# Top-k attention and Fourier mixing: in the first batch, the copies of P and the attention's pieces come a step later and the weight conversion comes last in ScalarE's step

## The chip, the cores and the metric

The kernel runs on one core of one Trainium2 chip, in float32. The metric is device microseconds of a whole execution. The core has a matrix engine (TensorE, PE), three engines for elementwise work (VectorE or DVE, ScalarE or ACT, GpSimd or POOL), and queues for DMA, nearly all of them issued by SyncE (SP).

## The reference, cut to what matters

```python
# attention: q, k, v of (8 batches, 8 heads, 576 tokens, 64)
scores = scale * np.matmul(q, k.transpose(0, 1, 3, 2))
kth = np.partition(scores, -32, axis=-1)[..., -32:-31]
scores = np.where(scores >= kth, scores, -1000000000.0)
attn = softmax(scores)
attn_out = np.matmul(attn, v)
# x: (8, 576, 512), heads side by side
mixed = np.real(fft(fft(x, axis=1), axis=2))
u = x + mixed
un = (u - mean(u)) / np.sqrt(var(u) + 1e-06)
out = u + np.maximum(un @ w_ch1, 0.0) @ w_ch2
```

w_ch1 has 512 x 2048 elements, w_ch2 2048 x 512. The weights arrive as 64-bit floats, which the kernel turns into float32 itself.

## The kernel before

**Tiles and steps.** The heads of a batch are worked in four pairs. A pair has nine tiles of query rows in the order `IN_PAIR` (line 301): for each head four tiles of 128 rows, and one that holds the last 64 rows of both heads. There are 288 tiles, and one loop (line 1394) runs over steps `i`, each of which issues different stages of several tiles; 36 tiles make a batch (`PER_BATCH`). The schedule is manual: every engine works its instructions in the order in which this loop writes them. Lists by step (`plan`, filled by `at(step, where, fn)`) hold the work that does not follow the tiles: weights, the Fourier transform, sums. A queue of matrix units of the last part (`mlp_units`) is drawn from between the fixed pieces by a budget per step; it is empty until batch 0 has been transformed.

**One tile.** `scores` (line 309) lets TensorE multiply q and k into two PSUM banks of the tag "sp" (two buffers) and ScalarE copy them to SBUF as S (L372), and in a second part the last 64 keys, the "tails" (L339, copies L343). `top_ops` (375) gives VectorE four rounds of the eight largest (L393) and their removal (L395); in step i it does rounds 2 and 3 of tile i interleaved with rounds 0 and 1 of tile i + 1. `bounds` (398) makes the tile's bounds on GpSimd (nt, L402). `mask` (406): ScalarE's relu (L409), then GpSimd's subtraction (L412). `expo` (414): ScalarE's exp with the row sum (L418), which reads what the subtraction wrote. `transposes` (423): TensorE turns P by blocks of 128 into one or two PSUM banks of the tag "tp" (two buffers; L439, L450, L454), and ScalarE copies them into PT (L442, L451, L455, L457). `attend` (461) multiplies PT with v (L476, 20 matmuls) in pieces: after tile 1 of a pair 128 columns, after tile 4 the other 192, after tiles 6 and 8 128 each. `attended` (482) copies the result to xT and prepares the reciprocals of the row sums (L490, L495, L502); `to_tokens` (507) turns it back (L516) and leaves the normalisation into x to VectorE (L503, L520, L527). `prep` (269) turns q or k of the next pair (L283; ScalarE's copies L291, L293, L297), q in step 0 of a pair (in step 2 for the first), k in step 5.

**The weights in batch 0.** 32 chunks of 128 x 512 come in by DMA (L186), five ahead; nearly every step of the first 34 works one. ScalarE makes three conversions (`convert`: L191, L207, L210), VectorE shifts the chunk of L191 (L199, `shift`, issued after round 3 of tile i), GpSimd joins the parts: L218 ahead of the mask's subtraction, L220 after it. In steps 19 and 27 (and 36 and 37) `centre` (1246) lets TensorE form column means in another bank of the tag "sp" (L1250). ScalarE copies the mean in the list "convert" of the next step (L1263), and GpSimd subtracts it from columns of the weights (L1259) in the four steps after.

**A step of the first batch** (`short`, steps 1 to 36). The loop issues, in this order: the conversions of step i; exp of tile i - 1; scores of the tile three ahead, and after them what `attended` left from the step before; preparations; means; score tails; transposes of tile i - 1 with their copies; `to_tokens`; the attention piece if tile i - 1 ends one; VectorE's rounds with the shift; the bounds and the mask of tile i. So ScalarE's order is: conversions (i), exp (i - 1), score copies, preparation, tails, copies of P (i - 1), relu (i). Later batches put the stages in other places, by the branches without `short`.

Of the kernel before, what the change touches and what calls it, by code (L numbers as in the profile page):

```python
# [18 lines left out]
P = 128  # L19
# [53 lines left out]
def kernel(  # L73
# [9 lines left out]
    nc = tc.nc  # L83
# [6 lines left out]
    NF = NC - 1  # L90
    TAIL = 2 * TH
# [10 lines left out]
    CW = (2 * P + TAIL, 2 * P)  # L102
# [199 lines left out]
    PER_PAIR = len(IN_PAIR)  # L302
# [117 lines left out]
            accum_out=den_t[pair % 3][:, c:c + 1],  # L420
        )

    def transposes(i):


        pair, t, e = items[i]
        p_sb = Wk.pop(i)
        ch, col = CHUNK_OF[t]
        if (pair, ch) not in PT:
            PT[pair, ch] = attp.tile(  # L430
                [P, 2 * NF + 1, CW[ch]], F32, name=f"PT_{pair}_{ch}", tag=f"PT{ch}", bufs=1
            )
        pt = PT[pair, ch]

        def full():
            k0 = TAIL if e == 1 else 0
            tp = ps_t.tile([P, 4, P], F32, name=f"tpP_{i}", tag="tp")
            for c in range(NF):
                nc.tensor.transpose(tp[:, c, :], p_sb[:, k0 + P * c:k0 + P * (c + 1)], ident)  # L439
            dsts = [(e, 0, P)] if e is not None else [(0, 0, TAIL), (1, TAIL, TAIL)]  # L440
            for he, o, w in dsts:
                nc.scalar.copy(  # L442
                    out=pt[:, NF * he:NF * (he + 1), col:col + w], in_=tp[:, :, o:o + w]
                )

        def tails():
            tp = ps_t.tile([P, 4, P], F32, name=f"tpP_{i}_t", tag="tp")
            if e == 1:
                both = Wp.pop(i - 1).rearrange("p e s -> p (e s)")[:, NF * P:S + TAIL]
                nc.tensor.transpose(tp[:, 0, :], both, ident)  # L450
                nc.scalar.copy(out=pt[:, 2 * NF, col:col + P], in_=tp[:, 0, :])  # L451
                return
            Wp.pop(i)
            nc.tensor.transpose(tp[:, 0, :], p_sb[:, S - P:S], ident)  # L454
            nc.scalar.copy(out=pt[TAIL:P, 2 * NF, col:col + TAIL], in_=tp[TAIL:P, 0, TAIL:P])  # L455
            for r in (0, TH):
                nc.scalar.copy(  # L457
                    out=pt[r:r + TH, 2 * NF, col:col + TAIL],
                    in_=tp[TAIL + r:TAIL + r + TH, 0, 0:TAIL],
                )  # L460

        full()
        if e != 0:
            tails()
        return 0.48 if e == 0 else 0.6

    def attend(pair, ch, c0=0, c1=None):

        c1 = CW[ch] if c1 is None else c1
        pt, vv = PT[pair, ch], v_of[pair]  # L470
        if c0 == 0:
            o_of[pair, ch] = ps_o.tile([P, CW[0]], F32, name=f"o_{pair}_{ch}", tag="o")
        o = o_of[pair, ch]
        for c in range(NC):
            for e in range(2):
                nc.tensor.matmul(  # L476
                    o[D * e:D * (e + 1), c0:c1],
                    lhsT=vv[:, c, e, :],
                    rhs=pt[:, 2 * NF if c == NF else NF * e + c, c0:c1],
                    start=(c == 0),  # L480
                    stop=(c == NC - 1),
                )
        return (c1 - c0) / 115.0
# [866 lines left out]
        at(arrivals[-1], "units", lambda b=b: (queue if b else waiting).extend(mlp_units(b)))  # L1350

    queue, waiting, pending, written, now, out_next = [], [], [], set(), [0], []
    step_us = 6.0

    def fixed_cost(i):
# [19 lines left out]
    def run(i, where):  # L1375
        for fn in plan.pop((i, where), []):
            fn()
# [16 lines left out]
    while i < N + 4 or plan or queue or sums:  # L1394
        now[0] = i
        run(i, "begin")
        pair_of = i // PER_PAIR

        short = 0 <= i - 1 < PER_BATCH
        done = i - 1 if short else i - 2 if PER_BATCH <= i - 2 < N else None  # L1400

        fixed, j = [], i + 3
        e = items[j][2] if j < N else None
        preps = []

        q_step = i == 2 if pair_of == 0 else i % PER_PAIR == 0
        if i < N and q_step:
            preps.append(lambda: prep("q", pair_of + 1))  # L1410
        if i < N and i % PER_PAIR == 5:
            preps.append(lambda: prep("k", pair_of + 1))
        fixed.append(lambda: scores(j - 1, 1) if e == 1 else scores(j, 0))
        n_mask = 0
        fixed += preps

        tok = []

        if pending and pending[0][0] <= i and (
            i < 2 * PER_BATCH + 4 or (i - 3) % PER_PAIR not in (4, 8)  # L1420
        ):
            _, pp, pc = pending[0]
            if pp // NPB < 2 or pp // NPB - 2 in written:
                pending.pop(0)
                tok.append(lambda: to_tokens(pp, pc, not short))
        if not short:
            fixed += tok
        for where in ("pe1", "pe2", "pe"):
            fixed += plan.pop((i, where), [])
        if e is None and j < N:  # L1430
            fixed.append(lambda: scores(j, 1))
        n_tr = len(fixed)
        if done is not None:
            fixed.append(lambda: transposes(done))
        if short:
            fixed += tok
            pair, r = divmod(i - 1, PER_PAIR)
            piece = {1: (0, 0, P), 4: (0, P, CW[0]), 6: (1, 0, P), 8: (1, P, CW[1])}.get(r)
            if piece is not None:
                fixed.append(lambda: attend(pair, *piece))  # L1440
            if i == PER_BATCH:
                fixed.append(lambda: attended(NPB - 1, 1, late_next) or 0.0)
                fixed.append(lambda: to_tokens(NPB - 1, 1, False))
        if i in arrivals:
            carry = min(carry, 0.0) if i > arrivals[0] else -5.0
            run(i, "units")
            step_us = level(i)
        room = step_us - carry - fixed_cost(i)
        cost, got = carry, 0.0
        run(i, "convert")  # L1450
        if short:
            expo(i - 1)
        for n, fn in enumerate(fixed):
            cost += fn()
            if n == n_mask:
                if PER_BATCH <= i - 1 < N:
                    mask(i - 1)
                run(i, "act")
                for fn in out_next:
                    fn()  # L1460
                out_next.clear()
            if n == min(n_tr, len(fixed) - 1) and PER_BATCH <= i - 1 < N:
                expo(i - 1)

            got += some(max(room * (n + 1) / len(fixed) - got, 1.1 if fn in preps else 0.0))
        if short:
            if piece is not None and r in (4, 8) and i < PER_BATCH:

                out_next.append(lambda pc=(pair, r // 8): attended(*pc, late_next))
                pending.append((i + 1, pair, r // 8))  # L1470

        soon_tile = 2 * PER_BATCH - 1
        for tile in (i - 3, i - 2):
            if not PER_BATCH <= tile < N or (tile == i - 2) != (tile == soon_tile):
                continue
            pair, r = divmod(tile, PER_PAIR)
            if r in (4, 8):
                cost += attend(pair, r // 8)
                attended(pair, r // 8, late_next)
                pending.append((i + 1, pair, r // 8))  # L1480
        if i < N:
            if q_step:
                load_nat("k", pair_of + 1)
            if i % PER_PAIR == 5:
                load_nat("q", pair_of + 2)
            if i % PER_PAIR == 6:
                load_v(pair_of + 1)
        first, second = top_ops(i, (2, 3)), top_ops(i + 1, (0, 1))
        for n in range(max(len(first), len(second))):
            for ops in (first, second):  # L1490
                if n < len(ops):
                    ops[n]()
                if ops is first and n == len(first) - 1:
                    run(i, "shift")
        if not first:
            run(i, "shift")

        planned = 1.5 * len(plan.get((i, "pool0"), [])) + 1.3 * len(plan.get((i, "pool2"), []))
        run(i, "pool0")
        some_sums(max(2.1 - planned, 0.0))  # L1500
        bounds(i)

        some_sums(1.3)
        if i < PER_BATCH:
            mask(i, lambda: run(i, "join"))
        for fn in late_now:
            fn()
        run(i, "dve")
        for where in ("pool", "pool2", "load", "load2"):
            run(i, where)  # L1510
        late_now[:] = late_next
        late_next.clear()
        carry = max(-4.0, min(4.0, cost + got - step_us))
        i += 1
# [36 lines left out]
```

## Time and profile before

| | |
|---|---|
| median of three runs | 1907.68 us (lowest 1907.42) |
| the profiled execution | 1907.16 us, of it the span 1905.4 us |
| TensorE busy (PE) | 1790.4 us, 94% |
| VectorE busy (DVE) | 1585.3 us, 83% |
| ScalarE busy (ACT) | 1208.5 us, 63% |
| GpSimd busy (POOL) | 908.4 us, 48% |
| relu L409, exp L418 of ScalarE, one each | 787 ns, 780 ns |
| subtraction L412 of GpSimd | 1416 ns |
| joins L218, L220 of GpSimd (first 220 us) | 1290 ns, 1298 ns |
| conversions L191, L207, L210 (first 220 us) | 663, 669, 665 ns |
| shift L199 of VectorE (first 220 us) | 608 ns in the mean, 32 times |

How to read it: busy time is a sum over the whole execution. Lines of a timeline give the start in us from the span's start, the duration in us, the engine, the line of the kernel, the operation, what it writes and what it reads; a bracket at the end gives how long the engine had been idle and what ended that. PEld is TensorE's loading of weights, beside the matmuls. Records of one engine may overlap by some tenths of a microsecond[...]: the starts, not the durations, give the rate.

### The profile page before, as it was taken

Reading aid. Unit: us, or ns where it says so; the run is one execution under the profiler, and the core shown is the slowest. Engines: PE = TensorE matmul, PEld = TensorE weight load, DVE = VectorE, ACT = ScalarE, POOL = GpSimd, SP = SyncE. Lnnn points to the kernel's source line nnn. Section 1 sums busy time; section 2 is a strip of 40 time slices with the busy share of each in tenths; the row PEclk is TensorE's granted clock in tenths of the full one; section 3 lists DMA queues with packets and bytes.
Section 4 is the critical chain, followed back from the end, with each engine's and each line's share of the span. In section 5 each row is a group of like instructions: output and inputs, shape, how many; then the busy total and the mean of one; then the engine's idle time right before and its main releaser. Section 6 shows DMA issues by size and latency. Waiting matters only on the chain.

```text
span 1905.4 us, 28704 instructions
## 1 busy us (share of the span) xinstructions
PE 1790.4 (94%) x9200; PEld 1182.4 (62%) x9200; DVE 1585.3 (83%) x3301; ACT 1208.5 (63%) x3078; POOL 908.4 (48%) x1278
## 2 busy tenths in 40 slices
PE   5567799999899999999999999999999999999999
PEld 3344465474567756667567656667567656667678
DVE  7999999999899999989899888989899888872110
ACT  6878657776766767657676667666676667652100
POOL 4768643556535374345534464245534464241022
PEclk7787899999999999999999999999999999999999
DMA  5333001311104111131113101141113102030132
GB/s 165 104 94 108 20 13 50 99 56 25 41 14 130 34 25 47 42 107 28 25 47 98 53 20 52 35 114 27 25 47 97 53 19 57 25 103 6 50 101 80
DMA packets 184342, 111.25 MB, mean 58 GB/s; under 512 B 125952, under 2 KB 174208, under 8 KB 184192
## 3 DMA queue, kind: packets, MB, share of 16 engines
q1 hardware_dynamic: 183408, 109.20, 20.3%
q8 instruction: 74, 1.21, 0.3%
q14 instruction: 76, 0.62, 0.1%
q10 hardware_dynamic: 784, 0.21, 0.0%
HBM read 93.63 MB, written 15.73 MB: 57 GB/s over the span
## 4 chain that ended last, share of the span: by engine, by line
PE 80%; ACT 8%; DVE 6%; POOL 3%; issue 1%; DMA 1%; SPq 1%; POOLq 0%; DVEq 0%; ACTq 0%
PE hp L878 26%; PE cp L905 10%; PE o L476 8%; PE tpP L439 6%; PE sp L369 5%; PE cw L1075 5%; PE cv L1075 4%; PE yp L667 3%; PE cp L944 3%; DVE m L393 2%; DVE wk L395 2%; PE sp_t L339 2%; PE mp L728 2%; POOL wk L412 1%; ACT wk L409 1%
## 5 line engine op out<-in xcount | busy, mean ns | idle before, releaser
L412 POOL TENSOR_TENSOR wk<-S,wk 128x576 f32<-128x576 f32 x288 | 407.7, 1416 | 731.8 <-ACT wk L409 701.2
L393 DVE MAX8 m<-wk 128x8 f32<-128x576 f32 x864 | 626.3, 749 | 6.1
L878 PE MATMUL hp<-unT,w 128*128 128x256 f32 (+1 forms) x2048 | 539.9, 410 | 2.6 <-ACT unT L796 2.6
L878 PEld LDWEIGHTS hp<-unT,w 128*128 128x128 f32 x2048 | 374.3, 191 | 124.7 <-issue 25.8
L395 DVE MATCH_REPLACE8 wk<-m,wk 128x576 f32<-128x576 f32 x576 | 427.6, 742 | 0.0
L418 ACT ACTIVATE wk<-wk,nt 128x576 f32<-128x576 f32 x288 | 224.7, 780 | 75.6 <-POOL wk L412 74.5
L409 ACT ACTIVATE wk<-S,nt 128x576 f32<-128x576 f32 x288 | 226.8, 787 | 36.2 <-POOL nt L402 35.2
L439 PE MATMUL tpP<-ident,wk 128*128 128x128 f32 x1152 | 183.9, 284 | 67.3 <-ACT wk L418 40.7
L905 PE MATMUL cp<-w,hT 128*128 128x512 f32 x512 | 240.6, 598 | 0.0
L442 ACT COPY PT<-tpP 128x512 f32<-128x512 f32 (+1 forms) x320 | 171.2, 547 | 106.8 <-PE tpP L439 104.3
L393 DVE MAX8 m<-S 128x8 f32<-128x576 f32 x288 | 214.0, 743 | 21.6 <-ACT S L343 21.6
L439 PEld LDWEIGHTS tpP<-ident,wk 128*128 128x128 f32 x1152 | 141.2, 145 | 141.2 <-ACT wk L418 64.2
L882 ACT ACTIVATE hT<-hp 128x320 f32<-128x320 f32 (+1 forms) x256 | 104.7, 409 | 194.5 <-PE hp L878 192.1
L395 DVE MATCH_REPLACE8 wk<-m,S 128x576 f32<-128x576 f32 x288 | 213.7, 742 | 0.0
L476 PE MATMUL o<-PT,v 128*64 128x256 f32 (+3 forms) x1440 | 195.2, 414 | 1.9 <-ACT PT L442 1.8
L372 ACT COPY S<-sp 128x512 f32<-128x512 f32 (+1 forms) x264 | 141.7, 588 | 48.9 <-PE sp L369 48.6
L369 PE MATMUL sp<-kT,qT 64*128 64x512 f32 (+1 forms) x528 | 160.2, 666 | 4.8 <-ACT means L1263 3.3
L476 PEld LDWEIGHTS o<-PT,v 128*64 128x64 f32 x1440 | 111.4, 152 | 73.8 <-issue 16.7
L905 PEld LDWEIGHTS cp<-w,hT 128*128 128x128 f32 x512 | 88.8, 190 | 86.3 <-issue 86.2
L1020 POOL TENSOR_TENSOR hT<-hT 128x512 f32<-128x512 f32 x64 | 81.4, 1275 | 100.3 <-ACT hT L882 88.6
L1075 PE MATMUL cw<-w,hT 128*128 128x256 f32 x448 | 106.7, 383 | 1.4 <-POOL nt L402 1.2
L1075 PEld LDWEIGHTS cw<-w,hT 128*128 128x128 f32 x448 | 81.4, 190 | 18.9 <-issue 5.2
(157 smaller groups left out, 2179.3 us busy)
## 6 DMA issues: line engine op xcount, KB each, us to landing
w<-w_parts SPq DMA_DIRECT2D x82, 512.0 KB, 4.4
space<-in_moe_w_ch_dram SPq DMA_DIRECT2D x32, 512.0 KB, 3.5
nat<-in_q_dram SPq DMA_DIRECT2D x128, 64.0 KB, 2.1
v<-in_v_dram SPq DMA_DIRECT2D x128, 64.0 KB, 2.2
out_dram<-x SPq DMA_DIRECT2D x32, 256.0 KB, 2.1
nat<-in_k_dram SPq DMA_DIRECT2D x124, 64.0 KB, 2.2
w_parts<-w_t SPq DMA_DIRECT2D x8, 512.0 KB, 2.9
w_s<-w_parts SPq DMA_DIRECT2D x8, 512.0 KB, 4.8
```

Of the source, the lines that this page charges most:

```text
L369: nc.tensor.matmul(sp[r], lhsT=qT[hd, q_cols], rhs=kT[hd, :], start=True, stop=True)
L393: ops.append(lambda src=src, m8=m8: nc.vector.max(out=m8, in_=src))
L395: ops.append(lambda src=src, m8=m8: nc.vector.match_replace(w, m8, src, NEG))
L409: nc.scalar.activation(out=w, in_=Ssb[i], func=AF.Relu, scale=-FAR, bias=Nt[i][:, 1:2])
L412: nc.gpsimd.tensor_tensor(out=w, in0=Ssb.pop(i), in1=w, op=ALU.subtract)
L418: nc.scalar.activation(out=w, in_=w, func=AF.Exp, bias=Nt.pop(i)[:, 0:1], accum_out=den_t[pair % 3][:, c:c + 1],)
L439: nc.tensor.transpose(tp[:, c, :], p_sb[:, k0 + P * c:k0 + P * (c + 1)], ident)
L442: nc.scalar.copy(out=pt[:, NF * he:NF * (he + 1), col:col + w], in_=tp[:, :, o:o + w])
L476: nc.tensor.matmul(o[D * e:D * (e + 1), c0:c1], lhsT=vv[:, c, e, :], rhs=pt[:, 2 * NF if c == NF else NF * e + c, c0:c1], start=(c == 0), ...
L878: nc.tensor.matmul(hp[:, 0:w], lhsT=w1[:, dt, P * it:P * (it + 1)], rhs=unT[:, dt, 0:w], start=(dt == 0), stop=(dt == NDT - 1),)
L905: nc.tensor.matmul(cp, lhsT=hT[:, it, P * n:P * (n + 1)], rhs=w2[:, it, :], start=(it == 0), stop=(it == NIT - 1),)
L1075: nc.tensor.matmul(dst, lhsT=h()[a][:, kc, :], rhs=rhs_of(kc), start=start and kc == 0, stop=kc == NK - 1, skip_group_check=True,)
```

## The change

It concerns steps 1 to 36. `transposes` can put its copies of P into a list `held` in place of issuing them. In a step, these held copies (those of tile i - 2) are issued right after the first score matmuls and their copies. The attention's piece follows tile i - 2 in place of i - 1, so it, `attended`, `to_tokens` and the normalisation come a step later; the piece and `to_tokens` now stand ahead of exp and the transposes of tile i - 1. The conversions of step i, and a mean's copy in the same list, come after all of these and so just ahead of relu of tile i. In step 36 the last tile is worked at once, with copies that are not held. ScalarE's order becomes: score copies, copies of P (i - 2), preparation, tails, exp (i - 1), conversions (i), relu (i). The instructions are the same in number and kind; VectorE's differ only in the normalisation's place, GpSimd's and SyncE's orders do not change, and from step 37 on no engine's order does.

```diff
-    def transposes(i):
+    def transposes(i, held=None):
...
+        def copy(**kw):
+            if held is None:
+                nc.scalar.copy(**kw)
+            else:
+                held.append(lambda: nc.scalar.copy(**kw))
...
-                nc.scalar.copy(
+                copy(
                     out=pt[:, NF * he:NF * (he + 1), col:col + w], in_=tp[:, :, o:o + w]
                 )
...
-        if done is not None:
+        if done is not None and not short:
             fixed.append(lambda: transposes(done))
         if short:
-            fixed += tok
-            pair, r = divmod(i - 1, PER_PAIR)
-            piece = {1: (0, 0, P), 4: (0, P, CW[0]), 6: (1, 0, P), 8: (1, P, CW[1])}.get(r)
-            if piece is not None:
-                fixed.append(lambda: attend(pair, *piece))
-            if i == PER_BATCH:
+            begun = held[:]
+            held.clear()
+            last_of = i == PER_BATCH
+
+            def copies():
+                for fn in begun:
+                    fn()
+                return 0.0
+            fixed.insert(1, copies)
+            for tile in (i - 2, i - 1) if last_of else (i - 2,):
+                if tile == i - 1:
+                    fixed.append(lambda: expo(i - 1) or 0.0)
+                    fixed.append(lambda: transposes(i - 1))
+                pair, r = divmod(tile, PER_PAIR)
+                piece = {1: (0, 0, P), 4: (0, P, CW[0]), 6: (1, 0, P), 8: (1, P, CW[1])}.get(r)
+                if tile >= 0 and piece is not None:
+                    fixed.append(lambda pair=pair, piece=piece: attend(pair, *piece))
+            if last_of:
+                fixed += tok
                 fixed.append(lambda: attended(NPB - 1, 1, late_next) or 0.0)
                 fixed.append(lambda: to_tokens(NPB - 1, 1, False))
+            else:
+                fixed += tok
+                fixed.append(lambda: expo(i - 1) or 0.0)
+                fixed.append(lambda: transposes(i - 1, held))
+                fixed.append(lambda: run(i, "convert") or 0.0)
...
-        run(i, "convert")
-        if short:
-            expo(i - 1)
+        if not short or last_of:
+            run(i, "convert")
...
-            if piece is not None and r in (4, 8) and i < PER_BATCH:
+            if i > 1 and piece is not None and r in (4, 8) and not last_of:
```

More of the change, by code (lines that the diff above doesn't have):

```diff
@@ L450, in tails @@
                 nc.tensor.transpose(tp[:, 0, :], both, ident)
-                nc.scalar.copy(out=pt[:, 2 * NF, col:col + P], in_=tp[:, 0, :])
+                copy(out=pt[:, 2 * NF, col:col + P], in_=tp[:, 0, :])
                 return
@@ L454, in tails @@
             nc.tensor.transpose(tp[:, 0, :], p_sb[:, S - P:S], ident)
-            nc.scalar.copy(out=pt[TAIL:P, 2 * NF, col:col + TAIL], in_=tp[TAIL:P, 0, TAIL:P])
+            copy(out=pt[TAIL:P, 2 * NF, col:col + TAIL], in_=tp[TAIL:P, 0, TAIL:P])
             for r in (0, TH):
-                nc.scalar.copy(
+                copy(
                     out=pt[r:r + TH, 2 * NF, col:col + TAIL],
@@ L1352 @@
     queue, waiting, pending, written, now, out_next = [], [], [], set(), [0], []
+    held = []
     step_us = 6.0
```

## The prediction

> **What bounds the kernel now.** I read the forty slices first, then busy times in stretches of the first batch, then VectorE's instructions one by one, then one step in order of time.
>
> ```profile
> PE   5567799999899999999999999999999999999999
> DVE  7999999999899999989899888989899888872110
> ACT  6878657776766767657676667666676667652100
> POOL 4768643556535374345534464245534464241022
> PEclk7787899999999999999999999999999999999999
> ```
>
> A slice is 47.6 us. The change touches steps 1 to 36 alone, which end near 230 us: the first five slices. There TensorE is half idle and VectorE full; from the sixth on TensorE is full. So two regimes: VectorE sets when batch 0 is ready, and from then on TensorE has a queue that it works off to the end. A microsecond won or lost on VectorE in batch 0 should move the end by a microsecond, and nothing else can.
>
> ```profile
> core 0: us, PE busy (x) PEld busy (x) DVE busy (x) ACT busy (x) POOL busy (x), PEclk, DMA share, GB/s
> 10.00:65.00 55.00, 32.55 (x152) 20.02 (x150) 54.17 (x112) 44.07 (x101) 35.10 (x34) 0.72 0.51 159
> 65.00:120.00 55.00, 34.19 (x187) 22.84 (x189) 54.17 (x112) 45.62 (x110) 38.46 (x38) 0.75 0.37 108
> 120.00:175.00 55.00, 38.47 (x190) 22.35 (x188) 52.90 (x106) 45.25 (x105) 43.39 (x41) 0.82 0.34 101
> 175.00:230.00 55.00, 38.20 (x189) 22.47 (x189) 54.00 (x113) 41.04 (x99) 41.23 (x52) 0.78 0.14 37
> ```
>
> VectorE is busy 215.25 of 220 us. In its whole first batch it waits for another engine once, for the weight conversion:
>
> ```profile
> L199 DVE TENSOR_SCALAR w<-w x32: 401/411/1403, 21.8 to 206.3; 128x512 int32<-128x512 int32 x32
> ...
> 129.68 1.20 DVE L199 TENSOR_SCALAR w<-w 128x512 int32<-128x512 int32 x1 [1.34 <-ACT w L191]
> ```
>
> What could be won is therefore small: this 1.34, and the excess of the 32 shifts over their minimum, 19.47 - 32 x 0.405 = 6.5 us. What could be lost is shown by one step in which nothing is late:
>
> ```profile
> 166.78 0.40 DVE L199 TENSOR_SCALAR w<-w 128x512 int32<-128x512 int32 x1
> ...
> 166.93 0.30 POOL L402 TENSOR_TENSOR nt<-m,cc 128x2 f32<-128x2 f32 x1 [1.08 <-DVE m L393]
> ...
> 167.26 0.78 ACT L409 ACTIVATE wk<-S,nt 128x576 f32<-128x576 f32 x1 [0.26 <-POOL nt L402]
> 167.31 1.29 POOL L218 TENSOR_TENSOR w<-w,space 128x512 int32<-128x512 int32 x1
> 167.94 0.67 ACT L191 ACTIVATE w<-space 128x512 f32<-128x512 f32 x1
> ...
> 168.56 1.42 POOL L412 TENSOR_TENSOR wk<-S,wk 128x576 f32<-128x576 f32 x1
> ...
> 170.01 0.78 ACT L418 ACTIVATE wk<-wk,nt 128x576 f32<-128x576 f32 x1 [0.26 <-POOL wk L412]
> ...
> 172.18 0.41 DVE L199 TENSOR_SCALAR w<-w 128x512 int32<-128x512 int32 x1
> ```
>
> With D for the shift's start: relu (L409) at D+0.48, POOL's join at D+0.53, its subtraction (L412) D+1.78 to 3.20, exp (L418) at D+3.23, next shift at D+5.40. Before the change the next step's three conversions (L191, L207, L210) run inside the hole between relu and exp, from D+1.16; the first is done at D+1.83, 3.6 us ahead of the shift that reads it.
>
> **What the Trainium skill says.** "Perfetto Trace Analysis", section "Identifying the Most-Contended Engine": for VectorE occupancy is a fair measure of the bound, for TensorE matmul busy time is not. Agreed: VectorE 98% in these windows. "PSUM — Partial Sum Buffer", section "Engine vs sequencer instructions": ScalarE, VectorE and GpSimd queues are strict FIFO. The trace agrees: at 127.39 ScalarE's copy had waited 2.92 us for TensorE, and relu and conversion came after it. "SBUF — State Buffer", section "SBUF: two separate sides": a GpSimd operation and a VectorE one in a two-port mode take a shared port pair exclusively. Agreed: at 105.58 the shift took 1.05 instead of 0.41 while a POOL join that began at 105.05 ran to 106.34. "TensorE: Matmul & The Clock Gate", section "What's actually happening": a TensorE that was idle runs at half clock. Agreed: four transposes (L439) take 1.11 us in some steps and 0.66 in others.
>
> **The change part by part.** *Copies of P a step later.* Same instructions. ScalarE's waits for the transposes (15.4 us, 19 times, in 10 to 232 us) go, since those transposes are a step old. ScalarE is not the bound, so this pays nothing itself. What comes late next is exp behind POOL: 1.42 us of subtraction, now covered by score copies and copies of P. *Attention pieces ahead of the transposes.* 20 matmuls, 2.5 us for 128 columns, 3.6 for 192. They wait for copies of P in the same step, and the transposes of this step, then the next step's score matmuls and ScalarE's score copies, queue behind them. *Normalisation a step later* (VectorE, 0.6 to 0.8 us, eight times): moved within a full engine, nothing. SP and POOL keep their order; what follows step 37 keeps it on every engine.
>
> *Conversion after exp.* This is the part that touches the bound. On time, exp and its read-out end for issue at D+4.0, L191 at D+4.66; the next shift stands at D+5.40. The margin falls from 3.6 to about 0.75 us. The hole from relu's issue (D+1.17) to exp (D+3.23), 2.06 us, must now hold everything else of ScalarE: score copies 0.96 (two of 0.58, overlapping), tails 0.2, copies of P 0.5 to 1.0, xT with den and rd 0.5 or 0.95, q or k preparation 0.6 or 0.9 (starts in the timeline). The sums are 0.84 to 1.96 over the nine steps of a pair: they fit, if TensorE has delivered. I followed the queues with the cold durations. Where an attention piece precedes, score matmuls come 1.7 to 2.6 us after D and exp runs 0.9 to 1.6 late, less the 0.75 of margin: stalls of about 0.4, 0.65, 0.15 and 1.0 in steps 1, 2, 5 and 7 of a pair, 2.2 a pair, with less in the first (about 1.6, where 0.45 comes from the q preparation's DMA at 24.4). Step 7 as the example, from D of step 6 (times before it relative to step 5's D): score copies and copies of P end at 3.4, the piece of 192 columns at 6.9, transposes and tail (1.5) at 8.0, which is 2.55 after step 6's D; score tails 3.1, their copies 3.4, xT, den and rd 4.35, copies of P 4.85, exp 5.7, L191 6.4, against a shift due at 5.4: 1.0. With the warm durations (0.66 for transposes, 1.8 for a piece) exp is at most 0.5 late and these stalls are nil.
>
> *The two column means (L1250).* In step 19 the score tails (L339) stand behind 3.67 us of matmul; ScalarE's tail copies wait for them, and now exp and conversion wait behind the copies. Cold: tails at D+7.1, exp 7.4, L191 done 8.9: VectorE stalls 3.0 (warm) to 3.6. In steps 20 and 28 the copy of the mean comes last as well, so its score bank is held a step longer and two score matmuls share the other: about 0.6 us of alternation each in front of exp, 0.7 to 1.35 in step 20, 1.5 to 3.4 in 28 (the second mean delays the transposes of 27 too).
>
> The sum, cold: pairs 1 and 2: 1.6 + 2.2; pair 3: 3.6 + 1.35 + 1.15 = 6.1; pair 4: 3.0 + 1.1 = 4.1 (no weight left for its last stall); 14.0. Warm: 3.0 + 0.7 + 1.8 = 5.5. Won: the 1.34 with its 0.8 of excess at 129.68, and of the other excess that of steps 3, 7, 11 and 16 (1.9 us, where ScalarE was late behind transposes) and about 1 of the rest; the column subtractions (L1259) keep POOL full in eight steps, and their excess stays. Together 5.0. Net +9 cold, +0.5 warm. TensorE is cold in most of the first 165 us by the durations, so I take +6. The profiled execution has a span of 1905.4 and 1907.16 in all, 0.5 below the median 1907.68: about **1914 us**.
>
> Not shown before: a conversion behind exp. Below it is bounded by nothing lost (all the excess and the wait gone, -7.8); above by 33 stalls of the largest size found in an ordinary step, 33 x 1.0, less 5: +28. Later bank release costs nothing where two score banks stay free, and up to the figures above where not.
>
> **The rivals.**
> - *Cover holds* (24%). ScalarE's 4.7 us a step fit 5.42, transposes are warm, and only step 19 stalls, 3.0 against 5 to 7.8 won: 1903 to 1907, say 1905. For it: ScalarE is busy 80% and waits 15.4 us for transposes. Against: one late step finds 0.75 us of margin, not 3.6.
> - *The ring closes* (4%): slower than before by over 2%. Relu, subtraction, exp and conversion make one loop through ScalarE and POOL: 0.78 + 1.42 + 0.95 + 1.78 = 4.93, with five hand-overs 5.3 against VectorE's 5.42. It decides from 0.2 us more in each loop if ScalarE's other work does not fit into POOL's 1.42: then every step costs the remainder, (2.0 + 0.45 + 0.15) - 1.42 = 1.2, and 33 x 1.2 = 40 us: 1947. Against: the average other work is 1.6, and the join holds the subtraction back anyway.
> - *Nothing moves* (12%): losses and gains equal within 2 us, 1906 to 1910.
> - *Stalls as I add them* (60%): 1909 to 1927.
>
> That VectorE stops being the bound is excluded by its 98%.
>
> **How the numbers follow.** The likeliest case gives 1914, its own range 1909 to 1927. For 8 in 10 I go down into the first rival, to 1903, and stop at 1927: left out are the ring (4%), some cold tail and gains beyond 4 us. Two per cent (38 us) is about what a measurement of this kernel tells from no change. A gain of 38 is out of reach, since VectorE has 8 to give (1%); a loss of 38 needs the ring (4%); 95% lie within.
>
> **What would show it.** VectorE's shift (L199 before) should wait for the first conversion (L191) not once but in some ten to fifteen steps, near 122 to 125 us by 3 us or more, and in sum 5 to 14. Its busy time beyond 0.405 should fall from 6.5 to some 3. ScalarE's waits for transposes ahead of copies of P should vanish, its waits for POOL ahead of exp grow from 8.5. The first batch's token transform, whose first matmul is at 234.30, should start about 6 us later, and everything after keep its length. I am wrong if VectorE shows no new waits, or if the time moves after 240 us.

## The result and the profile after

The changed kernel takes **1917.35 us** (median of seven runs) against 1907.42 us of the kernel before, run beside it: a ratio of **1.0049, 95% interval 1.0037 to 1.0061**, so 7 to 12 us slower and well within 2%. One of the seven runs of the kernel before took 2641.49 us; the ratio leaves it out. Run again later, beside E9 to E11 (E12), the change gave 1.0041 [1.0029, 1.0054]. The profiled execution took 1918.23 us, span 1916.4; that of before 1907.16.

First the stretches of the first batch, in the columns of the table shown for the kernel before:

```profile
10.00:65.00 55.00, 38.30 (x151) 22.55 (x149) 51.97 (x108) 42.41 (x99) 32.97 (x33) 0.75 0.51 158
65.00:120.00 55.00, 36.17 (x172) 23.73 (x172) 52.79 (x113) 45.75 (x107) 37.13 (x36) 0.65 0.35 105
120.00:175.00 55.00, 36.58 (x177) 20.85 (x176) 48.79 (x102) 44.65 (x104) 42.56 (x40) 0.75 0.30 91
175.00:230.00 55.00, 39.30 (x173) 23.38 (x172) 50.38 (x106) 40.59 (x95) 37.51 (x36) 0.64 0.17 47
```

VectorE, the third pair of columns, was busy 215.25 us in these 220 us and is now busy 203.95: it has holes in every stretch, and the largest in the two that hold the means. TensorE's granted clock is lower in three of the four (before 0.72, 0.75, 0.82, 0.78). The view of one source line says what the holes wait for: VectorE's shift.

```profile
L199 DVE TENSOR_SCALAR w<-w x32: 400/426/1071, 21.8 to 214.3; 128x512 int32<-128x512 int32 x32
  ACT w L191: 12.7, 12
```

Twelve shifts wait 12.7 us for the first conversion, where one had waited 1.34. The longest shift fell from 1403 to 1071 ns and their sum from 19.47 to 14.61 us. Before, 11 shifts took over 0.5 us; each began while a GpSimd operation of 1.3 or 1.4 us was running, and ended 0.28 us after it. In the change three do; of its late shifts, all but one (0.89 us) take 0.43 us. So the last shift starts at 214.3 and not at 206.3: 12.71 - 1.34 of waits, less 4.86 of durations, are 6.5 of the 8.0 us. The other 1.5 lie in the starts: a shift that is on time starts 0.67 us after the start of the search ahead of it (L393, 0.75 us long), a late one only after that search has ended. That is 0.08 us for each of 15 more late shifts, and 0.25 in waits too short for the view to list.

The largest single hole is step 19, here as a timeline over all engines:

```profile
123.07 3.67 PE L1256 MATMUL cm<-w,ones 128*128 128x512 f32 x8 [0.71 <-issue]
...
127.00 0.43 ACT L343 COPY S<-sp_t 64x64 f32<-64x64 f32 x2 [2.65 <-PE sp_t L339]
127.45 0.78 ACT L418 ACTIVATE wk<-wk,nt 128x576 f32<-128x576 f32 x1
...
128.23 0.66 ACT L191 ACTIVATE w<-space 128x512 f32<-128x512 f32 x1
...
128.92 0.43 DVE L199 TENSOR_SCALAR w<-w 128x512 int32<-128x512 int32 x1 [3.45 <-ACT w L191]
```

Read upward from the shift: it waited 3.45 us for a conversion, which had stood behind exp, which had stood behind copies of score tails, and these had waited 2.65 us for a matmul that could not start before the column mean's 3.67 us were over. Work of TensorE's reaches VectorE through ScalarE's queue, without any dependence between mean and shift.

The ordinary stall comes once a pair, in steps 6, 15, 24 and 33, 1.07 or 1.08 us each time. The queue of ScalarE in steps 32 and 33:

```profile
205.30 0.59 ACT L293 COPY kT<-tpk 128x512 f32<-128x512 f32 x1 [1.04 <-PE tpk L283]
...
206.23 0.78 ACT L418 ACTIVATE wk<-wk,nt 128x576 f32<-128x576 f32 x1
...
210.52 1.07 ACT L372 COPY S<-sp 128x512 f32<-128x512 f32 x2 [1.06 <-PE sp L369]
...
212.84 0.78 ACT L418 ACTIVATE wk<-wk,nt 128x576 f32<-128x576 f32 x1
```

The k of the next pair is prepared in step 32: its copy waits for TensorE, exp comes after it at 206.23, the transposes of this P after exp, the scores of step 33 after the transposes, and their copy waits 1.06 again; five copies of P and exp follow, and the conversion ends at 214.26 for a shift at 214.29. No attention piece is in this chain: that of 192 columns starts at 211.92, after it.

**Then the batch's end.** The token transform (yp) starts at 245.05 in place of 234.30, so 10.75 us late, although VectorE lost only 8.0. TensorE's queue, before:

```profile
213.19 2.46 PE L476 MATMUL o<-PT,v 128*64 128x128 f32 x20
215.58 1.13 PE L369 MATMUL sp<-kT,qT 64*128 64x512 f32 x4
...
218.56 3.60 PE L1250 MATMUL cm<-w,ones 128*128 128x512 f32 x8
...
227.32 3.70 PE L1250 MATMUL cm<-w,ones 128*128 128x512 f32 x8 [0.84 <-ACT S L361]
...
234.30 0.75 PE L667 MATMUL yp<-fs,fg 128*64 128x145 f32 x7
```

and after:

```profile
221.03 2.08 PE L369 MATMUL sp<-kT,qT 64*128 64x512 f32 x4
...
224.75 2.39 PE L482 MATMUL o<-PT,v 128*64 128x128 f32 x18 [1.03 <-ACT PT L439]
...
229.51 3.60 PE L1256 MATMUL cm<-w,ones 128*128 128x512 f32 x8
...
238.06 3.70 PE L1256 MATMUL cm<-w,ones 128*128 128x512 f32 x8 [0.84 <-ACT S L361]
...
245.05 1.14 PE L673 MATMUL yp<-fs,fg 128*64 128x145 f32 x8
```

Before, the piece of tile 33 ran ahead of the batch's last full score matmuls, in time that TensorE had to spare. After, it comes a step later, behind these scores, and waits 1.03 us for copies of P that stand behind the score copies in ScalarE's queue. The mean of step 36 therefore starts 15.2 us after the last shift (229.51 - 214.29) and not 12.3 (218.56 - 206.27). From it on everything is rigid: the last mean follows 8.6 to 8.8 us later, and the transform 7.0 us after the last mean's start, in both kernels (234.30 - 227.32 and 245.05 - 238.06). VectorE's fold of the tokens (sd) starts at 237.99 instead of 229.95, 8.0 late like the last shift, but no longer decides.

After that nothing is lost or won: the multiplications hp run from 255.9 to 1877.1 before and from 266.3 to 1887.6 after, 1621.2 and 1621.3 us.

### The profile page after: what moved, and what is told of

Same layout as the page of the kernel before. It is cut to its first block, busy times and chain, and to the rows that moved or that the text cites. A ratio compares the mean times of both kernels' runs of the same rounds, so it can differ in the third digit from the quotient of the medians.

```text
span 1916.4 us, 28700 instructions
## 1 busy us (share of the span) xinstructions
PE 1807.3 (94%) x9200; PEld 1190.4 (62%) x9200; DVE 1582.8 (83%) x3301; ACT 1211.7 (63%) x3078; POOL 906.9 (47%) x1278
## 4 chain that ended last, share of the span: by engine, by line
PE 82%; ACT 7%; DVE 5%; POOL 3%; DMA 1%; issue 1%; SPq 0%; POOLq 0%; DVEq 0%; ACTq 0%
PE hp L884 25%; PE cp L911 10%; PE o L482 8%; PE sp L369 6%; PE tpP L445 6%; PE cw L1081 5%; PE cv L1081 4%; PE yp L673 4%; PE cp L950 3%; DVE m L393 2%; DVE wk L395 2%; PE sp_t L339 2%; PE mp L734 1%; ACT wk L418 1%; ACT S L372 1%
## 5 line engine op out<-in xcount | busy, mean ns | idle before, releaser
L393 DVE MAX8 m<-wk 128x8 f32<-128x576 f32 x864 | 626.4, 749 | 6.1
L393 DVE MAX8 m<-S 128x8 f32<-128x576 f32 x288 | 214.0, 743 | 19.7 <-ACT S L343 19.5
L445 PE MATMUL tpP<-ident,wk 128*128 128x128 f32 x1152 | 188.9, 290 | 39.6 <-ACT wk L418 37.0
L437 ACT COPY PT<-tpP 128x512 f32<-128x512 f32 (+1 forms) x281 | 150.7, 548 | 94.7 <-PE tpP L445 92.4
L369 PE MATMUL sp<-kT,qT 64*128 64x512 f32 (+1 forms) x528 | 167.4, 690 | 4.7 <-ACT S L372 1.9
```

The lines of the kernel that those rows point to most:

```text
L369: nc.tensor.matmul(sp[r], lhsT=qT[hd, q_cols], rhs=kT[hd, :], start=True, stop=True)
L393: ops.append(lambda src=src, m8=m8: nc.vector.max(out=m8, in_=src))
```

## The experiments

**Theory A**: the change loses its time where a conversion that now comes last in ScalarE's step makes VectorE's shift wait. After E1 to E4 it had two costs: that one, some 8 us at the last shift, and TensorE's chain at the batch's end, 2.7 to 3 us later against VectorE. The rivals are named in each expectation. The kernel before, run beside each group on its chip, had medians of 1906.61 (E1 to E4), 1906.49 (E5 to E8) and 1906.15 us (E9 to E12). All kernels compute the whole reference.

In the table all but the ratio is from the profiled execution, in us: the last shift's start, the sum of the waits of shifts, the mean of step 36 counted from the last shift, the transform's start. E6, E7 and E8 have no mean in step 36. The profiled executions of E4, E5 and E9 were 2.6 to 3.1 us shorter than the medians of their kernels, the others within 2.2 us of theirs.

| | last shift | waits | mean after it | transform | ratio to before, 95% |
|---|---|---|---|---|---|
| before | 206.3 | 1.3 | 12.3 | 234.3 | 1 |
| the change | 214.3 | 12.7 | 15.2 | 245.1 | 1.0049 [1.0037, 1.0061] |
| E1 conversions first | 206.2 | 0.9 | 15.5 | 237.3 | 1.0015 [1.0006, 1.0024] |
| E2 conversions last alone | 258.7 | 57.0 | 11.4 | 286.3 | 1.0275 [1.0260, 1.0291] |
| E3 conversions a step ahead | 204.5 | 3.2 | 18.4 | 238.4 | 1.0019 [1.0008, 1.0030] |
| E4 tails before means | 211.4 | 9.7 | 13.1 | 240.0 | 1.0040 [1.0028, 1.0053] |
| E5 exp, conversions first | 203.8 | 1.2 | 14.2 | 233.8 | 1.0005 [0.9997, 1.0014] |
| E6 E1, third mean earlier | 205.5 | | | 237.8 | 1.0015 [1.0008, 1.0021] |
| E7 before, third mean earlier | 209.1 | 3.7 | | 241.2 | 1.0020 [1.0013, 1.0027] |
| E8 E3, E4, third mean earlier | 202.1 | 0.0 | | 231.9 | 1.0003 [0.9994, 1.0012] |
| E9 E5, end as before | 203.1 | 1.2 | 12.2 | 230.8 | 0.9982 [0.9975, 0.9990] |
| E10 exp first, conversions last | 244.3 | 42.6 | 13.7 | 273.6 | 1.0203 [1.0190, 1.0217] |
| E11 E9, tails before means | 203.3 | 1.0 | 12.2 | 231.1 | 0.9979 [0.9968, 0.9989] |
| E12 the change again | 214.5 | 12.5 | 14.9 | 245.5 | 1.0041 [1.0029, 1.0054] |

### E1: the change, with the conversions first again

```diff
-                fixed.append(lambda: run(i, "convert") or 0.0)
...
-        if not short or last_of:
-            run(i, "convert")
+        run(i, "convert")
```

> The change with one part undone: the conversions (and a mean's copy) stand first in ScalarE's step again; held copies of P, pieces a step later and exp after them stay. Theory A (the loss is VectorE's shift waiting for a conversion that now comes behind exp): the shift's waits fall from 12.7 us in 12 steps to under 1.5 us, the last shift comes at 204 to 207 us instead of 214.3, and the time is 1902 to 1909 us, ratio to before 0.997 to 1.001. Rival B (the loss is TensorE's order, pieces ahead of the transposes, whose lateness reaches VectorE in another way): waits of another kind appear and the time stays at 1913 us or more.

Measured: 1909.26 us, just over the span of theory A and under the rival's. The shifts wait 0.9 us, and the last starts at 206.17 like before's 206.27; also their durations are back (a sum of 19.57 us against 19.47). Yet the transform starts 3.0 us later than before, with VectorE's fold on time (229.83 against 229.95). So the conversion's place is the first and larger cost, and what is left, 2.9 us [1.1, 4.6], is lost behind VectorE. That E1 and the kernel before have the same shifts says also that the later copies and pieces in themselves cost VectorE nothing in sum.

### E2: the kernel before, with the conversions alone last

```diff
-        run(i, "convert")
         if short:
             expo(i - 1)
+            fixed.append(lambda: run(i, "convert") or 0.0)
+        else:
+            run(i, "convert")
```

> The kernel before with one part of the change alone: conversions last in ScalarE's step, just ahead of relu; exp stays first, copies of P, pieces and turning back stay where they were. Theory A: ScalarE now runs exp, score copies, copies of P that wait for this step's transposes, then the conversions; the first conversion ends some 7 us after the shift before, against 5.4 that there are, so the shift waits 1.2 to 2 us in nearly every one of 32 steps: 40 to 60 us slower than before, 1947 to 1967 us. Then the held copies are what makes conversions ahead of relu bearable. Rival B: the conversion's place costs little by itself, the time is under 1920 us.

Measured: 1959.29 us. 28 of the 32 shifts wait, 57.0 us in all, the worst 6.48 us. The same late conversion costs 52 us without the other parts of the change and 6.5 with them (the change against E1). What the other parts are worth is not seen in the change's own profile, since it has no row for stalls that did not occur.

### E3: the change, with the conversions of a chunk a step ahead

```diff
-at(s0 + 1, "convert", lambda n=n: scale_high(n))
+at(s0, "convert", lambda n=n: scale_high(n))
...
-at(s0 + 1, "convert", lambda n=n: rest(n))
+at(s0, "convert", lambda n=n: rest(n))
```

> The change with the same order on every engine, but each chunk is converted one step earlier than it is shifted (in step i the conversions for step i + 1 stand last, ahead of relu). Theory A: the margin grows by a step's 5.4 us, the shift waits under 1.5 us in all, the last shift comes at 204 to 208 us and the time is 1902 to 1909 us. Rival C (what costs is not the shift's wait but relu, subtraction and exp coming late behind the conversions): nothing changes by more than 2 us, 1915 to 1919 us.

Measured: 1910.18 us, a little over the span of theory A, with more waits than the 1.5 us that it allowed; the rival is excluded. The conversions still come last, but for the next step's shift. The waits fall from 12.7 to 3.2, and the last shift comes 1.8 us before before's. The transform nevertheless starts 4.1 us later than before, while VectorE's fold starts at 230.33, 0.4 later. E1 and E3 reach the same end of TensorE's chain (237.3 and 238.4) from different shifts: at the batch's end it is this chain that sets the time.

### E4: the change, with the score tails ahead of the means

```diff
+        if short and e is None:
+            fixed.append(lambda: scores(j, 1))
         for where in ("pe1", "pe2", "pe"):
             fixed += plan.pop((i, where), [])
-        if e is None and j < N:
+        if e is None and j < N and not short:
             fixed.append(lambda: scores(j, 1))
```

> The change, with the score tails ahead of the column means in TensorE's steps of the first batch. Theory A with the step 19 as I worked it out (tail copies behind 3.67 us of matmul): the shift's wait near 129 us falls from 3.45 to 0.7 us or less, the one near 184 us (step 28, 2.49 us) stays within 0.7 us, and the time falls by 2 to 4 us against the change, to 1913 to 1915.5 us. Rival D (the 3.45 come from elsewhere, the score copies or the bank that the mean holds): it stays over 2.5 us and the time within 1 us of the change.

Measured: 1913.65 us. The wait of step 19 is gone, which shows that the mean in front of the tails had made it; but that of step 20 grew from 0.86 to 2.71, so of 3.45 us only about half was kept, and the last shift comes 2.9 us earlier. (Step 28 has 1.30 in place of 2.49, but so has the change in its second profile, E12, with 1.27.) The transform comes 5.0 earlier: the mean of step 36 now follows the shift by 13.1 us in place of 15.2. In TensorE's timeline the order of the end is the change's, but 18 of the last piece's matmuls take 1.31 us where the change took 2.39, and the four transposes after them 0.66 where it took 1.12: 1.5 of the 2.1 us are the same work done faster, at a granted clock of 0.75 in 216.4 to 223.2 us against the change's 0.50 in 219.8 to 228.2. In the ratio the gain is not clear of noise: 1.0040, where the change has 1.0049 and, in E12, 1.0041.

### E5: conversions and exp first, the rest as changed

E1, and in it

```diff
         run(i, "convert")
+        if short and not last_of:
+            expo(i - 1)
...
-                fixed.append(lambda: expo(i - 1) or 0.0)
                 fixed.append(lambda: transposes(i - 1, held))
```

> The kernel before with only the copies of P held for a step and the pieces a step later: conversions and exp both stand first in ScalarE's step, as before the change. Theory A2 (two costs: the shift's wait, some 8 us on VectorE with what it saves elsewhere, and exp behind the score copies, which puts TensorE's chain at the end of the batch, transposes, column means of steps 36 and 37, score tails, token transform, 2.7 to 3 us later): both gone, the step-36 means start within 12.8 us of the last shift, the token transform within 1 us of the kernel before's 234.3, time 1904 to 1908 us. Rival B2 (held copies and later pieces delay that chain): the means start 14.5 us or more after the last shift and the time stays at 1909 to 1911 us.

Measured: 1907.37 us. The transform starts where it was expected, but not for the expected reason: the mean of step 36 comes 14.2 us after the last shift and not within 12.8, and the shift itself is 2.4 us earlier than before, since the durations of shifts sum to 17.11 in place of 19.47. So exp behind the score copies is 1.3 us of the longer chain (15.5 in E1), and 1.9 remained to be found.

### E6 and E7: the third mean moved to step 31

In both, the mean of the third chunk group is formed in step 31 in place of 36, and subtracted where it was; the fourth mean stays in step 37; E6 is E1 with that, E7 the kernel before with that.

```diff
-start_of[n1] + 2 + 8 * c if early else PER_BATCH - 2 + c, "pe",
+start_of[n1] + 2 + 8 * c if early else 31 if c == 2 else PER_BATCH - 2 + c, "pe",
...
-s0 = now[0] + 1 + dt if early else now[0] + 3
+s0 = now[0] + 1 + dt if early else PER_BATCH + 1 + c
```

> Conversion first (as in the experiment of that name), and the third column means moved from TensorE's step 36 to step 31, their subtraction left where it was. Theory A2: the chain ahead of the token transform is 3.6 us shorter, so its first matmul comes at 233.5 to 235.5 us in place of 237.3, where VectorE's folds bound it again, and the time falls by 2 to 3 us to 1906 to 1907.5 us. Rival E (the 3 us come from VectorE and GpSimd blocking each other in the folds, or from the cold clock): the time stays within 1 us of 1909.3.

> The kernel before with the same move of the third means. Theory A2: there VectorE's folds and TensorE's chain meet, so the token transform starts at most 1 us earlier than 234.3, and the time stays within 1.5 us of before. If TensorE's chain alone bound it, the gain would be 3 us.

Measured: 1909.2 and 1909.8 us. E6 gained nothing, as its rival had it; E7 lost 3.8 us [2.5, 5.1], more than its expectation allowed. The trace of E6 shows the mean that was left at the end, in TensorE's timeline:

```profile
228.67 5.83 PE L1256 MATMUL cm<-w,ones 128*128 128x512 f32 x8 [0.85 <-ACT S L361]
```

and the trace of E8, which has the same mean moved, shows it so:

```profile
224.94 3.70 PE L1256 MATMUL cm<-w,ones 128*128 128x512 f32 x8 [0.85 <-ACT S L361]
```

The same eight matmuls take 5.83 us in E6, and 3.70 in E8, in the change and in E1. The last two form another mean a step before. In the stretch 228 to 234 us of E6 the granted clock is 0.58; in E1's 230 to 236, where its last mean runs, it is 1.00. These clocks agree with what the prediction cites of the Trainium skill ("TensorE: Matmul & The Clock Gate", "What's actually happening"): half clock after idle time; here it cost 2.1 us. But that the missing neighbour made the mean cold is not shown: it is missing in E7 and E8 as well, and there the mean left takes 3.70 us, at a granted clock of 1.00. So in the profiled execution of E6 the clock took back what the move had won; in E7 something else was lost. Its moved mean waited 4.30 us for ScalarE's score copies and then ran cold itself (5.17 us); ScalarE's copies of P waited 5.21 us for the transposes behind it, and the shifts of steps 32 and 33 then 1.9. At the mean's old place, in step 36, TensorE stood idle for 3.44 us: there the mean had filled a wait for ScalarE. Whether the chain bounds the end was not decided by these two; E9 does that.

### E8: E3 and E4 together, means copied first, third mean moved

> The change with conversions a step ahead of their shift, score tails ahead of the means, a mean's copy first in ScalarE's step, and the third means in step 31: all the costs that I found taken away, the order that saves the shift's excess kept. Theory A2: the shift waits under 1.5 us in all, the last shift comes at 202 to 204.5 us, the token transform at 231 to 234.5 us, time 1901 to 1906 us, faster than both kernels. If it is not under 1907, something else is lost that I have not named.

Measured: 1906.92 us, beside 1906.49: no difference, and just outside the expectation. No shift waits at all, and the transform starts 2.4 us earlier than before (231.9). Of that the ratio shows nothing. The profiled execution is still 1.0 us shorter than that of before: the hp multiplications take 0.6 us longer (1621.8) and what follows the last of them 0.8. Why is open.

### E9: E5 with the batch's last steps ordered as before

From step 34 on copies of P are issued at once, and the piece of tile 33 is back in step 34.

```diff
-            for tile in (i - 2, i - 1) if last_of else (i - 2,):
-                if tile == i - 1:
+            direct = i >= PER_BATCH - 2 and not last_of
+            if direct:
+                tiles = (i - 2, i - 1) if i == PER_BATCH - 2 else (i - 1,)
+            else:
+                tiles = (i - 1,) if last_of else (i - 2,)
+            for tile in tiles:
+                if tile == i - 1 and direct:
+                    fixed.append(lambda: transposes(i - 1))
+                elif tile == i - 1:
...
-                fixed.append(lambda: transposes(i - 1, held))
+                if not direct:
+                    fixed.append(lambda: transposes(i - 1, held))
```

> E5 (conversions and exp first, the rest as changed) with the last three steps of the batch ordered as before: from step 34 on the copies of P are issued at once and the piece of tile 33 is in step 34 again. Theory A, second cost (TensorE's chain at the batch's end is late because a piece and its copies stand behind the last scores): the column mean of step 36 comes at most 12.5 us after the last shift (E5 14.2, before 12.3), the transform starts near 232 us, the time is 1 to 2.5 us under E5's: 1904 to 1906.5. Rival (the chain is set by something else, such as score copies or loads): the mean stays 14 us after the shift and the time within 0.7 us of E5's.

Measured: **1903.17 us**, 0.8 under the expected span. TensorE's queue at the end:

```profile
210.15 1.53 PE L482 MATMUL o<-PT,v 128*64 128x128 f32 x20
...
212.09 1.13 PE L369 MATMUL sp<-kT,qT 64*128 64x512 f32 x4
...
215.26 3.60 PE L1256 MATMUL cm<-w,ones 128*128 128x512 f32 x8
```

The piece is ahead of the scores again, at 1.53 us in place of 2.39 and more, and the mean comes 12.2 us after the last shift (203.08). The transform starts 3.0 us earlier than in E5, 0.8 from the shift and 2.2 from the chain. The second cost is thereby shown by putting it back. E9 is also **faster than the kernel before**, though by far less than 2%: 3.4 us [1.9, 4.8], last shift 3.2 earlier, transform 3.5 earlier. The durations of its shifts sum to 16.22 us, 3.25 under before's, as much as the last shift has gained: 8 of them, and not 11, take over 0.5 us, each again behind a GpSimd operation. Why the new order has fewer such meetings was not followed.

### E10: the change, with exp alone first

```diff
-                fixed.append(lambda: expo(i - 1) or 0.0)
                 fixed.append(lambda: transposes(i - 1, held))
...
         if not short or last_of:
             run(i, "convert")
+        if short and not last_of:
+            expo(i - 1)
```

> The change with exp first in ScalarE's step; the conversions stay last. Theory A (the shift waits because the conversion stands behind all that ScalarE does between relu and the end of its step, whatever it is): exp no longer waits for the score copies, but the conversions still do, and now follow an exp that POOL has delayed; the first conversion ends some 6.3 us after the shift before it instead of 5.4, the shift waits 0.3 to 1.5 us in most steps, 20 to 35 us in all, time 1925 to 1945. Rival (the copies of P of the same step alone make a late conversion costly, as in E2, and these are now a step old): like the change or better, at most 1920.

Measured: 1945.33 us, 0.3 over theory A's span and far from the rival's; the waits, 42.6 us in 27 steps, are larger than the 35 that theory A gave at most, with up to 2.17 us in an ordinary step. ScalarE's queue in step 32:

```profile
232.75 0.78 ACT L418 ACTIVATE wk<-wk,nt 128x576 f32<-128x576 f32 x1 [1.56 <-POOL wk L412]
...
233.72 0.59 ACT L439 COPY PT<-tpP 128x512 f32<-128x512 f32 x1
...
235.52 0.59 ACT L293 COPY kT<-tpk 128x512 f32<-128x512 f32 x1 [1.04 <-PE tpk L283]
...
236.45 0.67 ACT L191 ACTIVATE w<-space 128x512 f32<-128x512 f32 x1
```

exp first means that ScalarE does nothing while GpSimd subtracts: 1.56 us here, 47.9 in 31 steps of the first 232 us. In the change the same wait is 4.6 us in 7 steps, because score copies and copies of P fill it. All else then follows exp and stands in front of the conversion, which is ready 2.17 us after its shift could have started. The copies of P are a step old here, and a late conversion costs 38 us all the same (1.0203 against E5's 1.0005). So the change's own order, exp late and conversions last, is a matched pair: with conversions last, exp first costs 30 us more (1945.33 against E12's 1915.15); with conversions first, exp late costs about 2, not clear of noise (E1 against E5).

### E11 and E12: the best order with the tails, and the change again

E11 is E9 with E4's edit; E12 is the change itself.

> E9 with the score tails ahead of the column means in steps 19, 27 and 36. Theory A: with the conversions first no shift waits for tails, so little is left to win: TensorE's chain of the end is shorter by nothing, the time is E9's within 1 us, 1903 to 1906. Rival (the tails behind the mean still delay VectorE through scores not copied in time): 2 us or more under E9.

> The change itself once more, beside the kernel before on the same chip as the three others. Theory A: ratio 1.004 to 1.006. Rival (part of the difference is the chip's): a ratio under 1.003 or over 1.007.

Measured: 1902.33 us for E11, 0.9979 [0.9968, 0.9989], 0.7 under the expected span and not to be told from E9; 1915.15 us for E12, at the lower end of its span of ratios. With the conversions first no shift waits for tails any more, and the moved tails bring nothing. E12 repeats the sum of the change's waits (12.5), its shift (214.52) and its transform (245.53) within half a microsecond. Single waits differ more: 1.70 us in place of 0.86 in step 20, 1.27 in place of 2.49 in step 28. A difference of a microsecond in one stall between two kernels is therefore no effect by itself. E9 and E11 are the versions to keep: both beat both kernels.

With these runs the change can be taken apart by ratios of 0.001, each 1.9 us. From before to E9, copies and pieces a step later: 3.4 won. From E9 to E5, the same in the last steps too: 4.4 lost. From E5 to E1, exp behind score copies and copies of P: 1.9 lost. From E1 to the change, conversions behind exp: 6.5 lost. The intervals are 1.4, 2.2, 2.4 and 2.9 us on both sides, so the 1.9 of exp are not clear of noise by themselves; the starts of the transform in the traces go the same way, by -3.5, +3.0, +3.5 and +7.8.

## Why the prediction was right, and where it was not

The forecast was 1914 us, 6.3 above the median of before, in a range of 1903 to 1927; the change took 9.3 us more than before by its ratio. The likeliest case came, by its mechanism.

*VectorE is the bound of batch 0 and pays for late conversions.* Right. New waits stand at the shift, in twelve steps, 12.7 us in sum (expected: ten to fifteen steps, 5 to 14 us); E1 takes the conversion's place away and 8.1 us of shift start with it. The time of shifts beyond 0.405 us each fell from 6.5 to 1.7 us, more than the expected fall to some 3.

*"A microsecond won or lost on VectorE in batch 0 should move the end by a microsecond, and nothing else can."* The first half held: 8.0 at the last shift are 8.0 at the fold. The second half is **the step that failed**: 2.7 us were lost in TensorE's chain at the batch's end. The part "attention pieces ahead of the transposes" named what queues behind a piece, but priced it only through the next shift: the transform was to start about 6 us later, and started 10.75 later. After the last shift, that price is paid in full, with no VectorE to compare with. E1, E3 and E9 show it: on time in VectorE and 3.0 and 4.1 late, and back with the old order. That the range held is owed to its width here: the sum had no term for these 2.7 us.

*The sum: 14.0 lost cold, 5.5 warm, 5.0 won.* Measured, 12.7 lost and 4.86 + 1.34 won, with 1.5 of later starts: 8.0 net at the shift, near the cold end of +9. The mis-sized term is the choice between both: +6 was taken for a TensorE cold in most steps, and its granted clock then fell in three of four stretches. Why it fell was not tried. Step 19 took 3.45 (3.0 to 3.6 expected), step 20 0.86 (0.7 to 1.35), step 28 2.49 (1.5 to 3.4). The ordinary stalls were one a pair of 1.07 us and some of 0.2 to 0.5, where four were added up, the largest, of 1.0, in step 7 behind the piece of 192 columns. Size right, place wrong: it is in step 6, behind the preparation of k in step 5.

*ScalarE's waits.* Those for transposes ahead of copies of P vanished as said, 15.4 us to 2.9, all of it in step 36. Those for GpSimd ahead of exp were to grow from 8.5 and fell to 4.6. What came late next was TensorE's scores, as these two groups of the view of waits after show (in all, times, longest):

```profile
ACT S L372 <- PE sp L369: 17.7, 17, 2.2
ACT S L343 <- PE sp_t L339: 10.5, 9, 2.6
```

Before, they were 4.9 and 5.6 us.

*The rivals.* "Cover holds" needed one stall only; there were twelve. "Nothing moves" is excluded by the interval. "The ring closes" at 1947 did not occur in the change, but its two relatives ran: E10 at 1945 and E2 at 1959 have 27 and 28 stalled steps. The condition given, ScalarE's other work filling GpSimd's 1.42 us, was the right one: what keeps the ring open in the change is that exp stands behind that work.

*Everything after keeps its length*: right, 1621.2 and 1621.3 us from first to last hp.

## What to carry to other kernels

Where an in-order engine serves the bounding one, a late place for its work makes every earlier wait in its queue the bound's wait, whatever causes it; look for the longest such wait (here a mean of 3.67 us on a third engine), not for the mean load. Price a moved piece also at the end of its stage, where no bounding engine hides it and the next stage starts on its end: the chain from the last work of the bound to the first of the next stage is worth reading by itself. And take a bundle of moves apart: one part of this one won 3.4 us, the three others lost 4.4, 6.5 and some 1.9 (the last within noise), and the best order is neither kernel's.

## What the runs showed of the hardware

The same work of TensorE can take very different times at one place of the schedule: the eight float32 matmuls of 128 x 512 of the last mean took 5.83 us in E6 and 3.70 in E7 and E8, with the same neighbour moved away in all three. At the same place in the batch a piece of 20 matmuls with 128 columns took 1.53 us in E9 and 2.46 before. A difference of 1 or 2 us in one profile can thus be TensorE's clock alone.

A VectorE shift of 128 x 512 int32 took 0.40 to 0.46 us, or over 0.5 up to 1.48. In the 14 profiles all 95 shifts of over 0.5 us began while a GpSimd operation on the weights or the mask was running, and each ended 0.28 or 0.29 us after that operation. Behind a late conversion a shift met fewer of them, 3 in the change in place of 11: that is where the change won its 4.86 us.

From the first to the last hp, whose work is the same in all kernels, the profiled executions took between 1617.9 (E10) and 1621.8 us (E8), without a relation to the edits that I could find. A difference of 2 us in the length of two single profiles is therefore no effect by itself; the start of the transform together with the ratio is a better guide.
